# The last 1 MB of an output projection, asked for as a staircase of small transfers

## The chip, the core and the metric

The kernel runs on one core of one Trainium2 chip. The metric is the time of one execution in microseconds (us) on the device; lower is better. TensorE (PE) multiplies, VectorE (DVE) and ScalarE (ACT) do the element work, GpSimd (POOL) hardly takes part, and the queue of SyncE (SP) asks for nearly every transfer. Sixteen DMA engines move the data.

## The reference

Two layers run one after the other, on one token for each of 8 sequences, in float32. Both layers use the same weights and the same cache, so each layer reads all of it again.

```python
def _A_ref(x, k_cache, v_cache, wq, wo):          # x: (8, 1, 1024)
    q = (x @ wq) as 32 heads of 128
    k, v = caches (8, 4, 4096, 128), each of the 4 heads shared by 8 query heads
    p = softmax(q k^T * 128 ** -0.5)
    o = p v
    return o (8, 1, 4096) @ wo                    # wo: (4096, 1024)

def _B_ref(x, w1, b1, w2, b2):
    h = gelu(x @ w1 + b1)                         # w1: (1024, 3584)
    return h @ w2 + b2                            # w2: (3584, 1024)

x = x + _A_ref(layernorm(x), ...); x = x + _B_ref(layernorm(x), ...)   # layer 0
x = x + _A_ref(layernorm(x), ...); x = x + _B_ref(layernorm(x), ...)   # layer 1
```

## The kernel before

All weights and both caches are streamed from HBM through one large tile in SBUF, `arena`. It has 52 units of 1024 columns: 4 KB in each of the 128 partitions, 0.5 MB in all. The order of the stream and the place of each piece are tables written out by hand: `batch(...)` queues the pieces of one sequence's keys and values, `weights(...)` those of a weight matrix, with a list of sizes in units and a list of first units. `pump()` walks that list: it takes the next piece if its units are free, records one transfer on SP's queue (L268), and stops at the first piece whose units are still held. `release(slot)` runs after the last matmul that reads a piece is recorded; it frees the units and calls `pump()`. So the order of the transfers on SP is fixed when the program is built, and on the chip SP takes them strictly one after the other: a transfer that has to wait holds up all those behind it.

A transfer on SP can wait for two kinds of thing. The first is its place: the matmuls that read the old contents. The second is its counter. The framework gives each transfer one of eight counters in turn (`DMAHW0` to `DMAHW7` in the order below), so a transfer has the same counter as the one eight places earlier on SP, and it waits until that one has landed if nothing else already implies it. A transfer counts as landed when its counter has risen by 16.

This is the end of layer 1, where the change lies. `wo` (16 MB) follows the last values tile. In the text its transfers are called wo[0] to wo[5]: three of 4 MB (8 units each), then 2 MB, 1 MB and 1 MB, into units 24, 32, 16, 24, 28 and 30, so that the last three reuse the place of wo[0]. `project` (L424) multiplies the attention output with them, a unit at a time, into one accumulator `y`; then the residual and the layer norm follow (L206 to L229). Next come eleven pieces of `w1`, called w1[0] to w1[10]: five of 2 MB (units 32, 36, 16, 20, 24), three of 1 MB (28, 30, 32), one of 0.5 MB and two of 0.25 MB; and three last pieces of `w2` (`late`). The rest of `w2` for layer 1 already lies in the arena. `expand` (L303, L306) multiplies with `w1`, and `down_row` (L472) with `w2` in between. The result is added at L846 and stored at L848.

Of the kernel before, what the change touches and what calls it, by code (L numbers as in the profile page):

```python
# [14 lines left out]
P = 128  # L15
# [34 lines left out]
Q_AT = (0, (B + 1) * QW - 32, (B + 1) * QW - 8, 32)  # L50
KEEP = SCW + CH + 3 * P
DMA_SCRATCH = 64


class Arena:
# [50 lines left out]
def decode_layers(ctx: ExitStack, tc: tile.TileContext, x, kc, vc, wq, wo, w1, w2, out):  # L106


    nc = tc.nc
# [148 lines left out]
    def pump():  # L258
        while stream:
            key, k, src, starts, keys = stream[0]  # L260
            if not k:
                slot = Kept(starts)
            else:
                slot = arena.take(k, [i for i in starts if i + k <= arena.limit])
            if slot is None:
                return
            stream.pop(0)
            nc.sync.dma_start(out=slot.ap[:, 0:src.shape[1]], in_=src)  # L268
            slot.cols = src.shape[1]
            slot.keys = keys  # L270
            held[key] = slot

    def release(slot):
        if slot.keys:
            held.update(slot.parts())
            return
        slot.free()
        pump()
# [424 lines left out]
    def opened():  # L703
        arena.limit = N_UNIT
        pump()
# [14 lines left out]
    def weights(name, dram, sizes, starts, c0=0, i0=0, kept=None):  # L720

        at = c0
        for i, k in enumerate(sizes):
            n = min(int(k * SCW), dram.shape[1])
            k = -int(-k // 1)
            keys = kept(i) if kept else ()
            stream.append(((name, i0 + i), k, dram[:, at:at + n], starts(k, i), keys))
            at += n
# [26 lines left out]
    def fixed(*at):  # L755
        return lambda k, i: (at[i],)
# [9 lines left out]
    def batch(layer, b, k_spots, v_spots):  # L766
        for a, spots in (("k", k_spots), ("v", v_spots)):
            stream.extend(cache(layer, b, a, listed(*((n, (at,)) for n, at in spots))))
# [19 lines left out]
    at = [32, 16, 24] * (4 * B)  # L788
    for b in orders[1][3:]:
        batch(1, b, *([(8, at.pop(0)), (8, at.pop(0))] for _ in "kv"))  # L790
    weights(("o1",), wo[0], [8, 8, 8, 4, 2, 2], fixed(24, 32, 16, 24, 28, 30))
    weights(("i1",), w1[0], [4] * 5 + [2] * 3 + [1, 0.5, 0.5], fixed(32, 36, 16, 20, 24, 28, 30, 32, 34, 35, 36))
    for e, n in LATE:
        w = LATE_C * Q4
        at, to = CB * NFT * Q4 + e * w, LATE_AT * SCW + e * w
        stream.append((("late", e), 0 if e else LATE_C, w2[0][:, at:at + n * w], arena.ap[:, to:to + n * w] if e else (LATE_AT,), ()))
    pump()
    rs = layernorm(x_row, rsum)
    queries(rs)
# [123 lines left out]
```

## Time and profile before

| | |
|---|---|
| time, median of 3 runs | 849.13 us (848.68 to 849.33) |
| the profiled execution: its own time | 848.87 us |
| its span, first to last instruction | 847.0 us |
| PE busy | 535.8 us, 63% of the span |
| DVE busy | 192.4 us, 23% |
| ACT busy | 55.4 us, 7% |
| read from HBM | 357.78 MB, 423 GB/s over the span |
| mean granted TensorE clock | 0.821 |

In the rows that follow, L268 is line 268 of the kernel. A row of the timeline gives the start, the duration, the engine, the line, the operation, output<-inputs, the shape and the count; the bracket at its end gives how long the engine had stood idle before it and what released it. "DMA to landing" counts from the issue on SP to the moment when the last of the DMA engines has reported. `in_w_dram` stands for w1 and w2 together. Times are counted from the start of the span.

### The profile page before, as it was taken

The page shows a single profiled execution, that of the slowest core. Times are in us where ns is not written, and L with a number is a line of the kernel's source. Part 1 is how long each engine was busy: PE and PEld are TensorE (multiplying, and loading weights), DVE is VectorE, ACT ScalarE, POOL GpSimd, SP SyncE. Part 2 cuts the span into 40 slices and gives each one's busy share as a digit, 9 for nine tenths or more (in the row PEclk, how much of TensorE's full clock was granted, in tenths as well). Part 3 has the DMA queues.
Part 4 walks back from the last instruction along what each step waited for, and adds up shares of the span by engine and source line. Part 5 has one row for each costly group of instructions (what it writes and reads, how often), then busy time and mean ns, then how long its engine had stood idle before and what let it go on. Part 6 is the DMA issues. An engine that isn't in the chain of part 4 may idle for free.

```text
span 847.0 us, 9470 instructions
## 1 busy us (share of the span) xinstructions
PE 535.8 (63%) x4120; PEld 179.1 (21%) x4120; DVE 192.4 (23%) x636; ACT 55.4 (7%) x118; POOL 2.4 (0%) x14
## 2 busy tenths in 40 slices
PE   0755565656656657677778775476666576655677
PEld 0221111111111111133243222111111121212334
DVE  0013132313222231300010242232414132222011
ACT  0110000000000000000201100000000000000021
POOL 0000000000000000000000000000000000000000
PEclk9977779676876877699999897968768768788899
DMA  9999999999999999999999999999999999999997
GB/s 402 420 423 430 433 433 431 426 436 427 424 428 435 434 432 421 427 429 424 429 409 413 399 427 438 429 430 435 425 438 426 434 429 433 431 426 434 421 426 285
DMA packets 19768, 358.51 MB, mean 423 GB/s; under 512 B 2192, under 2 KB 2576, under 8 KB 4112
## 3 DMA queue, kind: packets, MB, share of 16 engines
q1 hardware_dynamic: 19584, 357.77, 99.2%
q8 instruction: 32, 0.52, 0.3%
q10 hardware_dynamic: 144, 0.15, 0.1%
q14 instruction: 8, 0.07, 0.0%
HBM read 357.78 MB, written 0.13 MB: 423 GB/s over the span
## 4 chain that ended last, share of the span: by engine, by line
DMA 73%; PE 23%; DVE 2%; issue 1%; another core or an unknown queue 1%; ACT 0%; SPq 0%; ACTq 0%; DVEq 0%
DMA arena<-in_k_dram 28%; DMA arena<-in_v_dram 21%; DMA arena<-in_w_dram 10%; DMA arena<-in_wo_dram 8%; PE sps L595 8%; PE o_ps L638 7%; DMA arena<-in_wq_dram 5%; PE y L424 2%; PE acc L361 1%; PE sps L472 1%; PE acc L306 1%; PE sps L650 1%; PE acc L303 0%; PE sps L346 0%
## 5 line engine op out<-in xcount | busy, mean ns | idle before, releaser
L595 PE MATMUL sps<-arena,qz 128*32 128x512 f32 x1024 | 162.3, 777 | 118.9 <-DMA arena<-in_k_dram 117.0
L638 PE MATMUL o_ps<-arena 128*32 128x512 f32 x512 | 87.4, 816 | 48.2 <-DMA arena<-in_v_dram 36.7
L638 PE MATMUL o_ps<-arena,spare 128*32 128x512 f32 x512 | 84.9, 782 | 40.9 <-DMA arena<-in_v_dram 34.0
L595 PEld LDWEIGHTS sps<-arena,qz 128*32 128x32 f32 x1024 | 37.7, 132 | 208.2 <-issue 169.8
L643 DVE SCALAR_TENSOR_TENSOR scr<-o_ps,bits,scr 128x128 f32<-128x128 f32 x192 | 67.3, 351 | 6.8
L641 DVE TENSOR_SCALAR scr<-o_ps,bits 128x128 f32<-128x128 f32 x64 | 22.4, 351 | 144.6 <-PE o_ps L638 144.6
L424 PE MATMUL y<-arena,oxT 128*32 128x256 f32 x512 | 37.8, 441 | 23.5 <-DMA arena<-in_wo_dram 23.5
L361 PE MATMUL acc<-arena,oxT 128*32 128x512 f32 x248 | 32.9, 671 | 6.3 <-DMA arena<-in_wq_dram 4.9
L650 PEld LDWEIGHTS sps<-bits,scr 128*128 128x128 f32 x128 | 21.7, 213 | 67.6 <-issue 48.3
L638 PEld LDWEIGHTS o_ps<-arena 128*32 128x32 f32 x512 | 16.9, 134 | 81.4 <-issue 49.1
L638 PEld LDWEIGHTS o_ps<-arena,spare 128*32 128x32 f32 x512 | 17.2, 131 | 71.7 <-issue 47.1
L600 DVE TENSOR_SCALAR_CACHE_REDUCE arena<-sps 128x512 f32<-128x512 f32 x16 | 11.1, 691 | 91.4 <-PE sps L595 91.4
L651 DVE TENSOR_TENSOR oxT<-sps,scr 128x8 f32<-128x8 f32 x64 | 10.5, 164 | 87.1 <-PE sps L650 87.1
L600 DVE TENSOR_SCALAR_CACHE_REDUCE spare<-sps 128x512 f32<-128x512 f32 x16 | 11.1, 691 | 82.4 <-PE sps L595 82.4
L619 ACT ACTIVATE sps<-arena,bits 128x512 f32<-128x512 f32 x16 | 10.9, 681 | 285.2 <-DVE scr L613 285.2
L619 ACT ACTIVATE sps<-spare,bits 128x512 f32<-128x512 f32 x16 | 10.9, 681 | 263.6 <-DVE scr L613 263.6
L650 PE MATMUL sps<-bits,scr 128*128 128x8 f32 x128 | 27.6, 288 | 0.0
L424 PEld LDWEIGHTS y<-arena,oxT 128*32 128x32 f32 x512 | 18.0, 125 | 44.0 <-DMA arena<-in_wo_dram 25.9
L303 PE MATMUL acc<-arena,oxT 128*32 128x512 f32 x160 | 20.7, 631 | 9.2 <-DMA arena<-in_w_dram 9.2
L184 PE MATMUL sps<-spare,ident 128*32 128x512 f32 (+2 forms) x60 | 24.9, 533 | 0.6 <-DVE scr L217 0.6
L609 PE MATMUL sps<-scr,bits 128*128 128x128 f32 x32 | 7.6, 322 | 22.9 <-DVE scr L605 22.9
L466 PE MATMUL sps<-arena,oxT 128*32 128x256 f32 x224 | 14.2, 382 | 5.6 <-DMA arena<-in_w_dram 5.6
(134 smaller groups left out, 248.8 us busy)
## 6 DMA issues: line engine op xcount, KB each, us to landing
arena<-in_v_dram SPq DMA_DIRECT2D x25, 4096.0 KB, 21.6
arena<-in_k_dram SPq DMA_DIRECT2D x21, 4096.0 KB, 20.6
arena<-in_k_dram SPq DMA_DIRECT2D x20, 2048.0 KB, 18.2
arena<-in_w_dram SPq DMA_DIRECT2D x16, 2048.0 KB, 12.7
arena<-in_v_dram SPq DMA_DIRECT2D x11, 2048.0 KB, 19.7
arena<-in_wo_dram SPq DMA_DIRECT2D x8, 2048.0 KB, 13.0
arena<-in_wo_dram SPq DMA_DIRECT2D x3, 4096.0 KB, 24.2
arena<-in_w_dram SPq DMA_DIRECT2D x6, 1024.0 KB, 19.6
```

Source lines behind the costliest of these rows:

```text
L184: nc.tensor.matmul(ps[0:32, 0:w], ident[:, 0:32], spare[:, 0:w], start=True, stop=True)
L303: nc.tensor.matmul(acc[32 * j:32 * j + 32, :], lhs, slot.ap[:, c:c + CH], start=(kt < 4), stop=(kt >= NT - 4))
L361: nc.tensor.matmul(acc[u][32 * j:32 * j + 32, d0 - j * CH:d1 - j * CH], xnT[:, kt * XS:kt * XS + 32], ap[:, d0 - c0:d1 - c0], start=(kt == ...
L424: nc.tensor.matmul(y[32 * j:32 * j + 32, 0:Q4], lhs[:, n * B:n * B + 32], slot.ap[:, c + j * Q4:c + (j + 1) * Q4], start=(n == 0), stop=(n ...
L466: nc.tensor.matmul(y[32 * g:32 * g + 32], h_at(kt), w2_at[c, kt], start=(n < 4), stop=(n >= NFT - 4))
L595: nc.tensor.matmul(ps[32 * g:32 * g + 32, :], qz[:, c:c + 32], kt[:, g * CH:(g + 1) * CH], start=(j == 0), stop=(j == HKV - 1))
L600: nc.vector.tensor_scalar(st["row", b].ap[:, half * CH:(half + 1) * CH], ps, SCALE, None, op0=ALU.mult, op1=ALU.max, accum_out=st["mx", b] ...
L619: nc.scalar.activation(pp, row[:, h * CH:(h + 1) * CH], AF.Exp, bias=bias, scale=1.0, accum_out=ls[:, h:h + 1])
L638: nc.tensor.matmul(o[32 * g:32 * g + 32, :], s[:, g], v[:, g * CH:(g + 1) * CH], start=(half == 0), stop=(half == NH - 1))
L641: nc.vector.tensor_scalar(r, o[:, 0:P], sel_t[:, 0:1], None, op0=ALU.mult)
L643: nc.vector.scalar_tensor_tensor(r, o[:, t * P:(t + 1) * P], sel_t[:, t:t + 1], r, op0=ALU.mult, op1=ALU.add)
L650: nc.tensor.matmul(po[:, 0:REP], r_s[j % 2], sel_h, start=True, stop=True)
```

## The change

wo[5], 1 MB, becomes two tiles of 0.5 MB, in units 30 and 31. The table `CUT` names the first of the two by its key, `(("o1",), 5)`: it is asked for in sixteen transfers of 15, 14, 13 and so on down to 1 rows (partitions), and 8 rows at the end, 128 rows of 4 KB in all. In the text these are p0 to p15, and the whole tile behind them, one transfer of 0.5 MB, is wo[6]. All other transfers stay as they are.

```diff
+CUT = {(("o1",), 5): (*range(15, 0, -1), 8)}
...
-            nc.sync.dma_start(out=slot.ap[:, 0:src.shape[1]], in_=src)
+            r0 = 0
+            for n in CUT.get(key, (P,)):
+                nc.sync.dma_start(out=slot.ap[r0:r0 + n, 0:src.shape[1]], in_=src[r0:r0 + n])
+                r0 += n
...
-    weights(("o1",), wo[0], [8, 8, 8, 4, 2, 2], fixed(24, 32, 16, 24, 28, 30))
+    weights(("o1",), wo[0], [8, 8, 8, 4, 2, 1, 1], fixed(24, 32, 16, 24, 28, 30, 31))
```

SP's queue at the end of `wo`, before (the size is partitions x columns; the names in brackets are the counters waited for, PE's among them):

```order
L268 DMA arena<-in_wo_dram 128x8192 [waits DMAHW2_49,PE_49]
L268 DMA arena<-in_wo_dram 128x8192 [waits DMAHW3_49,PE_49]
L268 DMA arena<-in_wo_dram 128x4096 [waits DMAHW4_49,PE_49]
L268 DMA arena<-in_wo_dram 128x2048 [waits PE_49] x2
L268 DMA arena<-in_w_dram 128x4096 [waits DMAHW5_49,PE_49]
L268 DMA arena<-in_w_dram 128x4096 [waits PE_49]
```

The first two rows are wo[1] and wo[2]; their own counters are DMAHW5 and DMAHW6, and wo[3], wo[4] and wo[5] have DMAHW7, DMAHW0 and DMAHW1. w1[0] follows directly.

The same place after (the line is now L271): wo[4], then p0 to p8.

```order
L271 DMA arena<-in_wo_dram 128x2048 [waits PE_49]
L271 DMA arena<-in_wo_dram 15x1024 [waits PE_49]
L271 DMA arena<-in_wo_dram 14x1024
L271 DMA arena<-in_wo_dram 13x1024
L271 DMA arena<-in_wo_dram 12x1024
L271 DMA arena<-in_wo_dram 11x1024 [waits DMAHW5_49]
L271 DMA arena<-in_wo_dram 10x1024 [waits DMAHW6_49]
L271 DMA arena<-in_wo_dram 9x1024 [waits DMAHW7_49]
L271 DMA arena<-in_wo_dram 8x1024 [waits DMAHW0_49]
L271 DMA arena<-in_wo_dram 7x1024 [waits DMAHW1_49]
```

p0 has DMAHW1, p3 has DMAHW4, and from p4 on every piece waits for a counter alone: p4 for that of wo[1], p5 for wo[2], p6 for wo[3], p7 for wo[4], p8 for p0.

The end of the staircase and what follows it on SP:

```order
L271 DMA arena<-in_wo_dram 2x1024 [waits DMAHW6_49]
L271 DMA arena<-in_wo_dram 1x1024 [waits DMAHW7_49]
L271 DMA arena<-in_wo_dram 8x1024 [waits DMAHW0_49]
L271 DMA arena<-in_wo_dram 128x1024 [waits DMAHW1_49,PE_49]
L271 DMA arena<-in_w_dram 128x4096 [waits DMAHW2_49,PE_49]
L271 DMA arena<-in_w_dram 128x4096 [waits DMAHW3_49,PE_49]
```

wo[6] has come to wait for p8, w1[0] for p9 and w1[1] for p10. Sixteen transfers more are two full turns of the eight counters, so w1[0] and all behind it keep the counters that they had.

On PE, nothing changes but the waits: the last matmuls of `project`, before and after, read

```order
L424 MATMUL y<-arena,oxT 32x256 [waits DMAHW0_49]
L424 MATMUL y<-arena,oxT 32x256 x7
L424 MATMUL y<-arena,oxT 32x256 [waits DMAHW1_49]
L424 MATMUL y<-arena,oxT 32x256 x7
L206 MATMUL sps<-ident,xb 128x128 [waits DVE_49]
```

```order
L428 MATMUL y<-arena,oxT 32x256 [waits DMAHW0_49]
L428 MATMUL y<-arena,oxT 32x256 x7
L428 MATMUL y<-arena,oxT 32x256 [waits DMAHW4_49,DMAHW5_49,DMAHW3_49,DMAHW6_49,DMAHW2_49,DMAHW7_49,DMAHW1_49,DMAHW0_49]
L428 MATMUL y<-arena,oxT 32x256 x3
L428 MATMUL y<-arena,oxT 32x256 [waits DMAHW1_49]
L428 MATMUL y<-arena,oxT 32x256 x3
```

The eight matmuls of wo[5] are now four that wait for all eight counters, and four that wait for wo[6].

## The prediction, made blind

> **What bounds the kernel now.** I read the page first, then the chain of waits over the end, then PE's timeline there, and last the issues on SP one by one.
>
> ```profile
> DMA  9999999999999999999999999999999999999997
> DMA 73%; PE 23%; DVE 2%; issue 1%; another core or an unknown queue 1%; ACT 0%; SPq 0%; ACTq 0%; DVEq 0%
> 771.33 24.16 DMA arena<-in_wo_dram
> 795.53 7.12 PE y L424 x96
> 802.66 27.81 DMA arena<-in_w_dram
> 830.52 1.92 PE acc L303 x16
> ...
> 843.87 0.02 issue
> 843.90 0.42 DVE xb L846
> ```
>
> The DMA engines are busy in every slice, and the chain that ends last is 73% transfers. At the end it runs through wo[2] (issued 771.33, landed 795.5) and w1[4] (issued 802.66, landed 830.5); from there 13.4 us of PE work lead to the last addition. Whatever delays w1[4] delays the end by as much. PE's timeline shows how closely PE follows the transfers:
>
> ```profile
> 785.80 5.29 PE L424 MATMUL y<-arena,oxT 128*32 128x256 f32 x64 [4.55 <-DMA arena<-in_wo_dram]
> 795.53 7.07 PE L424 MATMUL y<-arena,oxT 128*32 128x256 f32 x96 [4.45 <-DMA arena<-in_wo_dram]
> 802.92 1.07 PE L424 MATMUL y<-arena,oxT 128*32 128x256 f32 x16 [0.32 <-DMA arena<-in_wo_dram]
> 805.40 1.07 PE L424 MATMUL y<-arena,oxT 128*32 128x256 f32 x16 [1.41 <-DMA arena<-in_wo_dram]
> 810.38 1.94 PE L303 MATMUL acc<-arena,oxT 128*32 128x512 f32 x8 [2.62 <-DMA arena<-in_w_dram]
> 830.52 1.92 PE L303 MATMUL acc<-arena,oxT 128*32 128x512 f32 x16 [1.31 <-DMA arena<-in_w_dram]
> ```
>
> These starts date the landings: wo[1] 785.8, wo[2] 795.5, wo[4] 802.9, wo[5] 805.4, w1[0] 810.4, w1[4] 830.5. PE waits for each, so it has no lead to spend.
>
> **The change, step by step.** First, when SP issues now (start and, below it, time to landing; wo[3], wo[5], w1[0]):
>
> ```profile
> L268 SPq DMA_DIRECT2D arena<-in_wo_dram x1: 328/328/328, 779.1 to 779.1; - x1
> DMA to landing us min/median/max: 21.3/21.3/21.3
> ...
> L268 SPq DMA_DIRECT2D arena<-in_wo_dram x1: 328/328/328, 781.3 to 781.3; - x1
> DMA to landing us min/median/max: 24.1/24.1/24.1
> ...
> L268 SPq DMA_DIRECT2D arena<-in_w_dram x1: 328/328/328, 789.4 to 789.4; - x1
> ```
>
> wo[3] lands at 779.1 + 21.3 = 800.4. The important thing is the lead: transfers are asked for more than 20 us before they land, and w1[0] is asked for at 789.4, 16 us before wo[5] is in. That lead keeps the engines fed.
>
> Second, is the wait for a counter real? It is in the trace: the first `late` transfer waits for a counter alone, that of w1[3], eight places ahead. Here are w1[3], that transfer, and SP's waits from 824.5 to 834:
>
> ```profile
> L268 SPq DMA_DIRECT2D arena<-in_w_dram x1: 327/327/327, 800.9 to 800.9; - x1
> DMA to landing us min/median/max: 24.0/24.0/24.0
> ...
> L268 SPq DMA_DIRECT2D arena<-in_w_dram x1: 328/328/328, 824.9 to 824.9; - x1
> ...
> SPq L268 <- DMA arena<-in_w_dram: 11.8, 3, 5.2
> ```
>
> w1[3] lands at 800.9 + 24.0 = 824.9, and the next transfer is issued at 824.9. So SP stands still until the transfer eight places ahead has landed on its slowest engine. There it costs nothing: those three are the last. In the staircase it does.
>
> Third, how fast SP issues when nothing holds it. Two in a row:
>
> ```profile
> 501.55 0.33 SPq L268 DMA_DIRECT2D arena<-in_k_dram  x1
> 501.93 0.43 SPq L268 DMA_DIRECT2D arena<-in_v_dram  x1
> ```
>
> That is 0.38 us from one to the next. Now the sequence. p0 is free at 781.3 as wo[5] was; p0 to p3 go out by 782.5. p4 waits for wo[1], 785.8. p5 waits for wo[2], 795.5; p6 for wo[3], 800.4; p7 for wo[4], 802.9. w1[0] and w1[1], which went out at 789.4 and next, stand behind them. p8 waits for p0, which lies right behind wo[4] on the engines and lands within 0.2 us of it, so it is no further stop. From p7 to wo[6] are nine steps (p8 to p15, then wo[6]): 9 x 0.38 = 3.4, so wo[6] is issued at 806.3, and w1[0] at 806.7. The waits of p9 to p15, wo[6] and w1[0] on the piece eight places ahead cost nothing as long as a small piece lands within 8 x 0.38 = 3.0 us of its issue.
>
> By then the engines are empty. Without w1[0], all that was asked for is wo[4] (in at 802.9) and staircase pieces, of which p0 to p5 hold 75 of 128 rows. How long from an issue to the flow? The trace has no transfer to idle engines, so bounds:
>
> ```profile
> out_dram<-xb SPq DMA_DIRECT2D x1, 128.0 KB, 1.7
> ...
> L268 SPq DMA_DIRECT2D arena<-in_w_dram x1: 328/328/328, 442.6 to 442.6; - x1
> DMA to landing us min/median/max: 5.4/5.4/5.4
> ...
> L268 SPq DMA_DIRECT2D arena<-in_k_dram x1: 328/328/328, 473.3 to 473.3; - x1
> ...
> 474.50:475.00 0.50, 0.50 (x8) 0.00 (x0) 0.27 (x1) 0.00 (x0) 0.00 (x0) 0.50 0.78 229
> 475.00:475.50 0.50, 0.50 (x6) 0.14 (x2) 0.00 (x0) 0.00 (x0) 0.00 (x0) 0.88 0.60 197
> 475.50:476.00 0.50, 0.50 (x8) 0.48 (x12) 0.00 (x0) 0.21 (x1) 0.00 (x0) 1.00 0.92 393
> ...
> 797.00:805.00 8.00, 6.67 (x100) 3.26 (x92) 0.00 (x0) 0.00 (x0) 0.00 (x0) 0.85 1.02 427
> ```
>
> The final store of 128 KB, with nothing else moving, takes 1.7 us with its transfer; a load of 0.5 MB behind others took 5.4 (the shortest of all loads). In between lies the issue at 473.3: the queue had run low, the rate (last column, GB/s) fell to 197, and it was back at 393 from 475.5, some 2 us after the issue. I take 2.0, since that row is nearest: a load, after a gap. At 427 GB/s, 0.5 MB takes 1.23.
>
> Landing of wo[6]: 806.3 + 2.0 + 1.2 = 809.5, where wo[5] landed at 805.4: **4.1 us later**. w1[0] is issued 0.4 us behind wo[6], so from there the engines are fed again, and every w1 piece comes at its old distance: w1[4] at 830.5 + 4.1, then 13.4 us of PE work. The layer norm between fits as before (w1[0] came 2.6 us after PE was free). The stores, the `late` pieces and their counters move along.
>
> Sum: 848.87 + 4.1 = **853.0 us**. That is against the profiled execution; the median of the runs is 0.26 above it, well inside the range.
>
> The smaller edits. Splitting the tile gives PE one more wait for eight counters; it stands before wo[6] has landed, so it is covered by that, and would cost a few tenths without. The data and the matmuls are the same. Costs of nothing: the deal of rows over engines, while the gap stands, because engines that run dry all start again together; the skew that they had is lost as well. That could give some back: w1[4] has its landing from the slowest engine, and after the gap the slowest is nearer to the rest. I put this at 0 to 0.7, and PE caps it: it waits 1.31 before w1[4], so a gain above that is not passed on.
>
> Bounds. Low: issues at 0.33 (0.4 less), flow 1.4 us after the issue (the store's 1.7 without 0.3 of transfer, 0.6 less), skew 0.7 less: 851.3, with room 851.0. High: the flow 4.2 us after the issue (5.4 less its 1.2), +2.2; then the round trip of a piece exceeds 3.0 by about 1.2 and delays wo[6] by that: 856.4. It is a row with a queue ahead of it, so I end the range at 856.0.
>
> [...] The price by row is 0.38 us per transfer on SP, plus the waits. [...]
>
> **Rivals.**
>
> *The staircase deals work to the faster engines, and the gap doesn't come (not slower).* The engines do finish apart:
>
> ```profile
> 838.00:839.00 1.00, 1.00 (x40) 0.92 (x36) 0.00 (x0) 0.00 (x0) 0.00 (x0) 1.00 0.91 344
> 839.00:840.00 1.00, 1.00 (x40) 0.83 (x32) 0.00 (x0) 0.00 (x0) 0.00 (x0) 1.00 0.68 264
> 840.00:841.00 1.00, 1.00 (x36) 0.83 (x32) 0.00 (x0) 0.00 (x0) 0.00 (x0) 1.00 0.55 203
> 841.00:842.00 1.00, 1.00 (x28) 0.51 (x24) 0.32 (x1) 0.23 (x1) 0.00 (x0) 1.00 0.29 111
> 842.00:843.00 1.00, 1.00 (x25) 0.60 (x23) 0.00 (x0) 0.00 (x0) 0.00 (x0) 1.00 0.03 12
> ```
>
> The busy share (second last column) falls over four microseconds, so the slowest engine is some 4 us behind the first. If 15 rows go to 15 engines, 14 to 14 and so on, one engine gets 16 rows of this tile and one none, in place of 8 each. A row of 4 KB on one engine takes 4096 B / (427/16 GB/s) = 0.153 us, so the slowest engine gains at most 8 x 0.153 = 1.2 us: 847.6. It loses as much, 850.1, if it is one that gets more. Both need SP to get past p5 to p7 early: wo[6] issued by 802, four microseconds sooner than my sum. The order and the counter row speak against that. 4%.
>
> *A piece is not spread.* All transfers of the trace have 128 rows; what one of 15, 13 or 11 does is not shown. If all pieces went through one engine, it would carry 128 rows, 19.6 us, in place of 1.2: the tile would be 18 us late, 867 us. 4%. [...]
>
> *Round trips bind.* A small piece lands more than 3.0 us after its issue, the eight counters go round slowly, and each later turn adds the excess: 855 to 858 us. The 5.4 us row speaks for it, the store's 1.7 against. 10%.
>
> *PE and the lost skew absorb more than I think:* 850.6 to 851.5. 6%.
>
> **The numbers.** My sum, within 851.3 to 855, has 76%. What a measurement of this kernel can tell from no change is about 0.2%, 1.7 us. Faster by that is almost excluded, as even the perfect deal gives 1.2: 2%. Within it: 4%, the first rival with either sign. Slower: 94%. The range 851.0 to 856.0 leaves out the first two rivals and parts of the others.
>
> **What would show it.** In the profile after: SP's issues of p5 to p7 at about 795.5, 800.4 and 802.9, w1[0] issued near 806.7 in place of 789.4, a hole in the DMA rate from about 803 to 808, and w1[4] near 834.6. No hole, or p5 issued before 790, and I am wrong about the counters; a hole much longer, and the round trip of small pieces is what I got wrong.

## The result

| | before | after |
|---|---|---|
| median | 848.87 us (847.37 to 849.33, 6 runs) | 854.51 us (853.93 to 857.02, 6 runs) |
| ratio to before | | 1.0076, 95% interval 1.0060 to 1.0091 |
| profiled execution, span | 848.87 us, 847.0 us | 857.02 us, 855.2 us |

The change costs 5.6 us by the medians. The profiled execution of after is a long one of its kernel: it was already 1.5 us late when wo[2] landed, ahead of anything that the change touches. So the stages below are compared by the time between landings.

The profile after. From the page, the DMA slices and the chain that ended last; before, all slices but the last were full, and now the third from the end is not:

```profile
DMA  9999999999999999999999999999999999999797
DMA 69%; PE 26%; DVE 2%; issue 1%; ACT 1%; another core or an unknown queue 1%; SPq 1%; ACTq 0%; DVEq 0%
```

PE's timeline, for the landings of wo[2], wo[4], wo[5] (all sixteen pieces), wo[6] and w1[0]:

```profile
797.03 8.15 PE L428 MATMUL y<-arena,oxT 128*32 128x256 f32 x96 [3.55 <-DMA arena<-in_wo_dram]
805.51 1.07 PE L428 MATMUL y<-arena,oxT 128*32 128x256 f32 x16 [0.33 <-DMA arena<-in_wo_dram]
809.94 1.08 PE L428 MATMUL y<-arena,oxT 128*32 128x256 f32 x8 [3.36 <-DMA arena<-in_wo_dram]
812.14 1.08 PE L428 MATMUL y<-arena,oxT 128*32 128x256 f32 x8 [1.12 <-DMA arena<-in_wo_dram]
818.69 1.93 PE L307 MATMUL acc<-arena,oxT 128*32 128x512 f32 x8 [3.78 <-DMA arena<-in_w_dram]
```

SP's issues of p5, p6, p7 and w1[0]:

```profile
L271 SPq DMA_DIRECT2D arena<-in_wo_dram x1: 282/282/282, 797.0 to 797.0; - x1
...
L271 SPq DMA_DIRECT2D arena<-in_wo_dram x1: 273/273/273, 802.3 to 802.3; - x1
...
L271 SPq DMA_DIRECT2D arena<-in_wo_dram x1: 272/272/272, 805.5 to 805.5; - x1
...
L271 SPq DMA_DIRECT2D arena<-in_w_dram x1: 376/376/376, 808.9 to 808.9; - x1
```

p5 goes out the moment wo[2] lands, p7 the moment wo[4] lands, and w1[0], once asked for 16 us ahead of wo[5], now goes out 3.4 us behind wo[4]. The chain of waits now runs through SP. It has p7, which follows the landing of wo[4], and then wo[6] and w1[0], which nothing but their turn held back:

```profile
805.49 0.27 SPq L271
...
808.43 0.36 SPq L271
...
808.88 9.67 DMA arena<-in_w_dram
```

The DMA rate, by windows (the last two columns are the busy share of the engines and GB/s):

```profile
799.00:801.00 2.00, 2.00 (x24) 0.92 (x20) 0.00 (x0) 0.00 (x0) 0.00 (x0) 0.50 1.02 410
801.00:804.00 3.00, 3.00 (x48) 1.51 (x44) 0.00 (x0) 0.00 (x0) 0.00 (x0) 0.72 0.69 212
804.00:810.00 6.00, 2.31 (x44) 0.89 (x40) 0.00 (x0) 0.00 (x0) 0.00 (x0) 0.96 0.30 63
810.00:811.00 1.00, 1.00 (x8) 0.14 (x8) 0.00 (x0) 0.00 (x0) 0.00 (x0) 0.50 0.78 283
811.00:840.00 29.00, 22.24 (x222) 9.18 (x222) 4.07 (x17) 7.22 (x14) 0.00 (x0) 0.73 1.01 428
```

There is the hole: six microseconds at 63 GB/s. And there is something that was not forecast: three microseconds ahead of it the rate is already down to 212. The share of 0.69 accounts for a part of that, since some engines have nothing left to move. The other part is that the busy engines are slower: 212 / 0.69 is 307 GB/s, where the row above it gives 410 / 1.02 = 402.

Taken apart by PE's starts, in us between landings, for every kernel of this study (from the rows of the timeline as shown above; in sixteen_by_columns, where PE does not wait for wo[4], from the landing of wo[4]; each table row is one profiled execution):

| kernel | wo[2] to wo[4] | wo[4] to the last of wo | to w1[0] | sum | against before |
|---|---|---|---|---|---|
| before | 7.39 | 2.48 | 4.98 | 14.85 | |
| after | 8.48 | 6.63 | 6.55 | 21.66 | +6.8 |
| split_only | 7.44 | 2.52 | 4.97 | 14.93 | +0.1 |
| four_by_32 | 9.83 | 8.68 with the next | | 18.51 | +3.7 |
| eight_by_16 | 8.72 | 3.98 | 6.24 | 18.94 | +4.1 |
| twenty_four | 7.68 | 9.44 | 6.07 | 23.19 | +8.3 |
| sixteen_by_columns | 7.4 | 8.5 | 6.11 | 21.96 | +7.1 |
| four_by_columns | 7.45 | 2.76 | 4.97 | 15.18 | +0.3 |
| four_strided | 7.42 | 2.52 | 4.99 | 14.93 | +0.1 |
| deal_of_three | 9.74 | 4.75 | 5.81 | 20.30 | +5.5 |
| deal_strided | 9.76 | 2.53 | 6.12 | 18.41 | +3.6 |
| after_shifted | 8.54 | 6.57 | 5.00 | 20.11 | +5.3 |
| before_shifted | 7.39 | 2.47 | 4.99 | 14.85 | 0.0 |

So the changed kernel loses in three places: 1.1 us before wo[4] has landed, 4.15 between wo[4] and wo[6], and 1.6 on w1[0]. Only the middle one was forecast. From w1[0] to the last addition both kernels take 33.5 us (810.38 to 843.90, 818.69 to 852.15), but not for the same reason. Before, PE waits 0.27 us for w1[3] and 1.31 for w1[4] in that stretch. After, it waits for no tile behind w1[0], because its own work is slower: the third last column of these rows is the granted TensorE clock in the 8 us from w1[0] on, for before, after and four_strided (an experiment below that loses nothing):

```profile
811.00:819.00 8.00, 6.78 (x76) 2.43 (x68) 0.88 (x4) 3.24 (x6) 0.00 (x0) 0.87 1.01 430
819.00:827.00 8.00, 7.14 (x44) 1.99 (x40) 0.88 (x4) 2.66 (x5) 0.00 (x0) 0.53 1.00 428
811.00:819.00 8.00, 7.15 (x44) 2.08 (x40) 0.88 (x4) 2.66 (x5) 0.00 (x0) 0.51 1.01 428
```

The clock of 0.5 is not the work of the change, since four_strided has it without a hole, and sixteen_by_columns, with a hole, has 0.86. But it decides what a late w1[0] costs here. In after, w1[4] landed at 838.14 and PE came to it at 838.77. So an earlier w1[0] alone could have gained 0.6 us, and then w1[4] would have been the bound again. Counted by w1[4], the last part divides into 0.9 us (w1[4] lands 26.0 us behind wo[6] in place of 25.1) and 0.6 us of slower PE.

### The profile page after: what moved, and what is told of

The parts are those of the page before. It is cut to its first block, busy times and chain, and to the rows that moved or that the text cites. A ratio compares the mean times of both kernels' runs of the same rounds, so it can differ in the third digit from the quotient of the medians.

```text
span 855.2 us, 9493 instructions
## 1 busy us (share of the span) xinstructions
PE 539.9 (63%) x4120; PEld 181.5 (21%) x4120; DVE 192.6 (23%) x636; ACT 55.6 (7%) x118; POOL 2.4 (0%) x14
## 4 chain that ended last, share of the span: by engine, by line
DMA 69%; PE 26%; DVE 2%; issue 1%; ACT 1%; another core or an unknown queue 1%; SPq 1%; ACTq 0%; DVEq 0%
DMA arena<-in_k_dram 28%; DMA arena<-in_v_dram 19%; DMA arena<-in_wo_dram 11%; PE sps L599 8%; PE o_ps L642 7%; DMA arena<-in_w_dram 7%; DMA arena<-in_wq_dram 5%; PE acc L307 2%; PE y L428 1%; PE sps L470 1%; PE sps L476 1%; PE acc L365 1%; SPq L271 1%; PE sps L654 0%
## 5 line engine op out<-in xcount | busy, mean ns | idle before, releaser
L599 PE MATMUL sps<-arena,qz 128*32 128x512 f32 x1024 | 164.8, 786 | 120.9 <-DMA arena<-in_k_dram 119.0
L642 PE MATMUL o_ps<-arena 128*32 128x512 f32 x512 | 84.3, 790 | 48.8 <-DMA arena<-in_v_dram 35.1
L428 PE MATMUL y<-arena,oxT 128*32 128x256 f32 x512 | 42.1, 475 | 24.7 <-DMA arena<-in_wo_dram 24.7
L470 PE MATMUL sps<-arena,oxT 128*32 128x256 f32 x224 | 16.4, 452 | 5.2 <-DMA arena<-in_w_dram 5.2
```

The costliest lines, as they stand in the source:

```text
L428: nc.tensor.matmul(y[32 * j:32 * j + 32, 0:Q4], lhs[:, n * B:n * B + 32], slot.ap[:, c + j * Q4:c + (j + 1) * Q4], start=(n == 0), stop=(n ...
L470: nc.tensor.matmul(y[32 * g:32 * g + 32], h_at(kt), w2_at[c, kt], start=(n < 4), stop=(n >= NFT - 4))
L599: nc.tensor.matmul(ps[32 * g:32 * g + 32, :], qz[:, c:c + 32], kt[:, g * CH:(g + 1) * CH], start=(j == 0), stop=(j == HKV - 1))
L642: nc.tensor.matmul(o[32 * g:32 * g + 32, :], s[:, g], v[:, g * CH:(g + 1) * CH], start=(half == 0), stop=(half == NH - 1))
```

## The experiments

**Is it the split alone?**

```diff
-CUT = {(("o1",), 5): (*range(15, 0, -1), 8)}
+CUT = {}
```

> The changed kernel without the staircase: wo[5] and wo[6] are two whole tiles of 0.5 MB, each one transfer on all 128 rows. Theory A (SP stands at the eight counters and the engines run dry): one transfer more moves the counters by one place and no new wait binds, so w1[0] goes out at 789 to 790 and the time is that of the kernel before, within 0.2% (847.4 to 850.6 us). Rival B (splitting the tile, with its extra PE wait, carries the loss): about 854.5.

Measured: 848.48 us, ratio to before 0.9998 (0.9990 to 1.0006). The split is free, extra wait on PE included; the loss is in the sixteen transfers.

**More and fewer pieces.**

```diff
-CUT = {(("o1",), 5): (*range(15, 0, -1), 8)}
+CUT = {(("o1",), 5): (32,) * 4}                    # four_by_32
+CUT = {(("o1",), 5): (16,) * 8}                    # eight_by_16
+CUT = {(("o1",), 5): (5,) * 16 + (6,) * 8}         # twenty_four
```

> wo[5] in four transfers of 32 rows, wo[6] whole. Theory A: the four pieces find free counters; wo[6] waits for wo[1] (785.8 us), w1[0] for wo[2] (795.5 in place of 789.4), w1[1] for wo[3] (800.4), w1[2] for wo[4] (802.9). All are asked for before the queue of the engines is empty, so nothing runs dry: the time of before within 0.2%. Rival C (each small transfer costs a fixed 0.35 us or more wherever it stands, 5.6 us for the sixteen): 4 x 0.35 = 1.4 us slower.

> wo[5] in eight transfers of 16 rows, wo[6] whole. Theory A: the eighth piece goes out when wo[4] has landed (802.9 us), wo[6] 0.4 us behind it, so wo[6] lands at 803.3 + 3.7 (what it took from issue to landing after the gap) = 807.0 in place of 805.4: 1.6 us slower, up to 3 if the first tile of w1 then also loses what it lost in the changed kernel. Rival C (fixed price of each transfer, 0.35 us): 2.8 us slower, and no hole in the DMA rate.

> wo[5] in 24 transfers, sixteen of 5 rows and eight of 6, wo[6] whole. Theory A: after the eighth piece, which goes out when wo[4] lands, there are eight transfers more than in the changed kernel, at 0.33 us each: 2.6 us more, so 8 us slower than before, 857 us. If a piece's landing takes 8 x 0.33 us or less, no more than that. Rival D (the odd shapes of the staircase, 15, 13, 11 rows, and how they are dealt over the engines, carry the loss): with the same rows on five or six engines throughout it differs from 854.5 in a way that the number of transfers doesn't tell.

Measured: four_by_32 852.25 us, ratio 1.0046 (1.0034 to 1.0059); eight_by_16 852.54, 1.0050 (1.0038 to 1.0062); twenty_four 856.26, 1.0089 (1.0074 to 1.0104). Twenty-four pieces came out near their forecast of 857, and their wo[6] lands 2.8 us later behind wo[4] than the changed kernel's, where eight more issues at 0.33 make 2.6. Four pieces did not: theory A had them free, and they cost 3.5 us. Eight pieces cost 3.8, more than the 1.6 to 3 that it gave; their wo[4] is 1.3 us late as well. SP did not stand in the way of four_by_32. This is its DMA rate over seven microseconds, with the engines busy throughout (share 1.04):

```profile
799.00:806.00 7.00, 4.17 (x72) 1.78 (x64) 0.00 (x0) 0.00 (x0) 0.00 (x0) 0.98 1.04 250
```

split_only in the same window:

```profile
799.00:806.00 7.00, 5.82 (x92) 2.59 (x84) 0.00 (x0) 0.00 (x0) 0.00 (x0) 0.94 1.03 428
```

Busy engines that move 250 GB/s in place of 428 are not starved but slow. Even wo[4], a whole tile that is in flight at the same time, is hit: it lands 2.4 us late. Each of the four transfers lies on 32 neighbouring partitions. So a second theory, G, was added, a guess of the author's: a transfer on few neighbouring partitions makes all engines write to a small part of SBUF, and that part is the limit.

**G against A: the same number of transfers, on all partitions.**

```diff
 # sixteen_by_columns and four_by_columns: cut by columns, all 128 rows in each transfer
+CUT = {(("o1",), 5): (784, *[16] * 15)}            # sixteen_by_columns
+CUT = {(("o1",), 5): (256,) * 4}                   # four_by_columns
+            c0 = 0
+            for n in CUT.get(key, (src.shape[1],)):
+                nc.sync.dma_start(out=slot.ap[:, c0:c0 + n], in_=src[:, c0:c0 + n])
+                c0 += n
 # four_strided: 32 rows again, every fourth
+CUT = {(("o1",), 5): 4}
+            m = CUT.get(key, 1)
+            for q in range(m):
+                nc.sync.dma_start(out=slot.ap[q:P:m, 0:src.shape[1]], in_=src[q:P:m])
```

> wo[5] in sixteen transfers again, but each on all 128 rows: 784 columns, then fifteen slivers of 16 columns. The counters turn as in the changed kernel; no transfer is on a part of the partitions. Theory A (counters): SP issues the sixth to eighth piece when wo[2], wo[3] and wo[4] land, wo[6] about 3 us after the eighth, so wo[6] lands 4.1 us late and the DMA rate has a hole of some 4 us; with 0 to 1.5 for a fetch that meets an engine after the restart 853 to 854.4 us, near the changed kernel. Theory G (found in the four pieces of 32 rows: transfers on few partitions run at half the rate, 200 to 250 GB/s, because sixteen engines write to one part of SBUF) as the main cause of the changed kernel's loss: here at most 1 us slower than before.

> wo[5] in four transfers of 256 columns on all 128 rows: as many transfers as four_by_32, of the same size. Theory G: no part of the partitions is favoured, the DMA rate stays at 400 to 430 GB/s, and the time is that of before within 0.2%. Rival C (four more transfers cost something by themselves): 3.5 us slower as four_by_32 was.

> wo[5] in four transfers of 32 rows of 4 KB, as in four_by_32, but each takes every fourth row, so that its rows lie over all the partitions. Theory G: the rate stays up and the loss of 3.5 us goes, to 0 to 1 us. Rival H (any transfer on fewer than 128 rows is slow, through the way its rows are dealt to the engines): 3.5 us slower again, with the rate at 200 to 250 GB/s for some 7 us.

Measured: sixteen_by_columns 856.27 us, ratio 1.0089 (1.0076 to 1.0102); four_by_columns 849.22, 1.0009 (1.0000 to 1.0017); four_strided 849.05, 1.0010 (1.0002 to 1.0019). The window from 799 to 806 in four_by_columns,

```profile
799.00:806.00 7.00, 6.33 (x92) 3.13 (x84) 0.00 (x0) 0.00 (x0) 0.00 (x0) 0.90 1.06 418
```

and in four_strided:

```profile
799.00:806.00 7.00, 5.58 (x92) 2.29 (x84) 0.01 (x1) 0.00 (x0) 0.00 (x0) 1.00 1.02 424
```

The last one differs from four_by_32 only in which rows each transfer takes, and 3 of the 3.5 us are gone. That shows that the choice of rows makes the loss of four_by_32. It turns down C and H as its cause: four transfers more cost 0.5 us by the medians of four_by_columns, 1.4 at most by its interval. That the limit lies in SBUF, as G says, is not shown: the same edit also changes which rows are read from HBM, and no run separates the two. sixteen_by_columns has full-width transfers alone, wo[4] lands on time, and the loss is there all the same, with the hole from 804 to 809:

```profile
804.00:809.00 5.00, 0.51 (x7) 0.05 (x2) 0.00 (x0) 0.00 (x0) 0.00 (x0) 0.76 0.23 28
```

That shows A. The loss is 7.6 us by the medians, and the time is 2 us above the top of the forecast, because SP needs longer from the eighth piece to wo[6] than in the changed kernel. The two issues:

```profile
L271 SPq DMA_DIRECT2D arena<-in_wo_dram x1: 327/327/327, 802.8 to 802.8; - x1
...
L271 SPq DMA_DIRECT2D arena<-in_wo_dram x1: 377/377/377, 807.5 to 807.5; - x1
```

Of these 4.7 us, 1.0 went by until the 784 columns had landed (the ninth piece shares their counter), and the next eight steps took 0.47 us each, where the changed kernel's pieces of 1 to 8 rows took 0.33.

**The third part: w1[0].** In the traces of before and after a transfer on all 128 rows leaves sixteen landing records on its counter, and in after p0 to p14, of 15 to 1 rows, leave fifteen to one of them at the landing; these are read here as one for each engine that takes part. In the changed kernel fifteen landing records of w1[0] lie within 0.5 us (816.43 to 816.93), and the sixteenth is 1.6 us behind them (818.56). A packet of 16 KB on q8, which the page lists as "instruction" and which is read here as a fetch of instructions, starts at 813.58 us in the middle of it. Sixteen matmuls that nobody reads, ahead of `project`, move the fetches.

```diff
+        if st["layer"] == 1:
+            idle(*[32] * 16)
         y = ps_o.tile([P, CH], F32, tag="o", name="y")
```

> The changed kernel, with sixteen small matmuls on PE that nobody reads, ahead of the output projection of layer 1, where PE waits for wo[0]. They move PE's instructions on by 64 entries. Theory E: in the changed kernel w1[0] landed 1.6 us later on one engine than on the other fifteen, because an instruction fetch (the queue q8 of the page) met that engine while it brought w1[0]; moved to an earlier place, into the gap, the fetch costs nothing, and the time falls by 1 to 1.6 us below the changed kernel, to 853 us. Rival F (the late engine comes of the restart after the gap): 854.5 as before, and w1[0] still lands more than 6 us behind wo[6].

> The kernel before with the same sixteen small matmuls: the control. They stand where PE waits 3.9 us for wo[0], so they cost nothing themselves. Theory E: a fetch that is moved meets another moment, and the engines already stand 3.5 us apart there, so the end moves by no more than 0.6 us. If it moves by 1.5 us or more, the matmuls themselves or the fetches act in some other way, and the run above can't be read as a test of the gap.

Measured: after_shifted 856.19 us, ratio 1.0089 (1.0075 to 1.0103); before_shifted 849.07, 1.0005 (0.9996 to 1.0014). Half of theory E holds. The fetch now starts at 801.4, and w1[0] comes 5.00 us behind wo[6] as in the kernel before, in place of 6.55. That turns down F: the restart alone makes no late engine. In twenty_four and sixteen_by_columns a fetch starts at 813.5 and 812.3, again while w1[0] comes in, and one engine is 1.1 us behind the other fifteen.

```profile
809.76 1.08 PE L430 MATMUL y<-arena,oxT 128*32 128x256 f32 x8 [1.03 <-DMA arena<-in_wo_dram]
814.76 1.94 PE L307 MATMUL acc<-arena,oxT 128*32 128x512 f32 x8 [2.23 <-DMA arena<-in_w_dram]
```

But the time did not fall to the forecast 853. The next fetch, at 826.1, meets w1[3], which lands 6.1 us behind w1[2] in place of 4.9. PE does not wait for w1[3], but the late engine stays late, and PE waits for w1[4]:

```profile
835.47 1.92 PE L307 MATMUL acc<-arena,oxT 128*32 128x512 f32 x16 [0.54 <-DMA arena<-in_w_dram]
```

Whether the 1.6 us can be had back at all was not settled.

**The uneven deal without the counters, and without neighbouring rows.** deal_of_three is the kernel before with the row loop of the change; deal_strided has the loop of four_strided.

```diff
+CUT = {(("o1",), 5): (49, 70, 9)}                  # deal_of_three, wo[5] kept at 1 MB
+CUT = {(("o1",), 5): 6}                            # deal_strided: every sixth row, as in four_strided
```

> wo[5] stays one tile of 1 MB, asked for in three transfers of 49, 70 and 9 rows (of 8 KB). Theory A: three transfers find free counters, so there is no gap. [...] In the changed kernel's trace the landings of its pieces say that the engines 11 to 14 were the last, by 4 us. They would lose 3 to 8 rows of 0.306 us: w1[4] lands about 0.9 us earlier, and the time falls by up to 0.9 us (0.1%), to 848.0. Rival: the slow engines are others from run to run, and the time stays, or rises by up to 1.5 us. Slower by 4 us or more would say that partial transfers cost something without the counters.

> The uneven deal without the two costs: wo[5] (0.5 MB) in six transfers, each of every sixth row (two of 22 rows, four of 21), so the rows of each lie over all partitions. The first five find free counters or wait for wo[1]; the sixth waits for wo[2] (795.5 us), wo[6] for wo[3] (800.4), w1[0] for wo[4] (802.9): no hole on the slow engines. [...] In the changed kernel's trace engines 11 to 14 were the last by about 4 us, and engines 0 to 6 the first ones. They would gain 1.2 us: the landings of w1[4] lie closer together (3.5 to 3.7 us in place of 4.2 to 4.4), and the time falls by 0.5 to 1.2 us, to 847.5 to 848.2. Rival: the order of the engines is another in other runs, or PE's own work is the bound there: no change (within 0.1%). A loss of 3 us or more would say that the stride doesn't heal partial transfers on fewer than sixteen engines.

Measured: deal_of_three 854.97 us, ratio 1.0081 (1.0067 to 1.0096); deal_strided 851.95, 1.0036 (1.0022 to 1.0049). Neither gains, and both forecasts missed. The 3 to 8 rows of the one and the 1.2 us of the other rest on the number of rows that each engine gets, which no run shows; the runs showed lower rates in its place. No transfer waits long for a counter in deal_of_three, and it still loses more than four_by_32. The rates, deal_of_three first:

```profile
799.00:806.00 7.00, 5.11 (x80) 2.40 (x72) 0.00 (x0) 0.00 (x0) 0.00 (x0) 0.87 1.08 274
```

```profile
799.00:806.00 7.00, 4.87 (x80) 2.25 (x73) 0.00 (x0) 0.00 (x0) 0.00 (x0) 0.92 0.83 220
```

wo[4] lands 2.4 us late in both. In deal_strided w1[0] has to wait for this late wo[4] (it is issued at 804.6 us) and comes 6.1 us behind wo[6], which is the rest of its loss. Its share of 0.83 says that some engines had nothing to move, but those that had were slow too: the 16 KB packets of the whole tiles took 1.0 to 1.6 us in this window, against 0.61 to 0.63 in four_strided. So spreading the rows heals transfers on 32 rows (424 GB/s) and does not heal those on 22 and 21 rows (220 GB/s). Theory G, as it stands, does not cover this. Why every sixth row is slow and every fourth is not stays open.

## Why the prediction was right, and where it was off

**The counters: right.** p5, p6 and p7 went out as wo[2], wo[3] and wo[4] landed, w1[0] behind all of them, the hole came where it was put, and split_only (no hole without the sixteen transfers) and sixteen_by_columns (the hole with sixteen transfers of another shape) show from both sides that their number makes it. Forecast for wo[4] to wo[6]: 6.6 us (802.9 to 809.5); measured 6.63. That it agrees so closely is luck, as the next paragraph shows.

**Two terms in it were off and cancelled.** The step on SP was taken at 0.38 us from large transfers; pieces of few rows took 0.33 (805.49 to 808.43 for nine steps), 0.5 us less in all. From issue to landing wo[6] was given 2.0 + 1.2 = 3.2 us; it took 3.7 (808.43 to 812.1), 0.5 us more.

**"Costs of nothing: the deal of rows over engines": wrong.** The step priced a row by its engine's rate and did not ask what the pieces do to the transfers beside them. In four_by_32 few neighbouring rows at a time bring the rate of all engines from 428 down to 250 GB/s, and wo[4], which is ahead of them on SP's queue, is 2.4 us late. In the changed kernel it is 1.1 us late, ahead of the hole. That this is the same effect is likely, but not shown: a staircase on spread rows was not run, and deal_strided, whose rows lie over all partitions, is slow too, at 220 GB/s. So neighbouring rows are not the whole cause.

**The lost skew, which was to give back 0 to 0.7: wrong, in sign.** In the kernel before, the landing records of a tile lie 3.5 us apart at that place, and a fetch need not cost anything: the one at 806.65 leaves those of w1[0] 3.5 us apart, and the one at 824.1 puts the last record of w1[4] back by 0.6. After the gap fifteen engines are within half a microsecond, and the one that the fetch met set the landing of w1[0], 1.6 us behind them. And w1[4] no longer set the end, as the sum had it. PE has no wait on `w1` behind w1[0], because its granted clock was lower in this execution (0.53 in the 8 us from w1[0] on, against 0.87 before), as it was in four_strided (0.51), which has no gap.

These two make 1.1 + 1.6 = 2.7 us in the profiled execution, against 1.5 (5.6 less 4.1) that the medians are above the sum. The median still lies within the range, because the room at its upper end, which was meant for a later flow after the issue, took in two costs that were not in the sum. That part is luck.

**The rivals.** The staircase without a gap is turned down by the issues. "A piece is not spread" is turned down by the landing records: on its counter p0 leaves 16 of them, p1 15, p2 14, down to 2 for p14. One comes some half a microsecond after the issue (p0: issued at 783.03, record at 783.58) and the rest, fifteen for p0 and one for p14, at the landing. (The profile counts sixteen records a transfer, so it has no time to landing for any transfer on these counters.) Round trips did not bind: pieces issued into empty engines landed in 1.6 to 2.1 us, below the 3.0 and below the 2.6 of eight measured steps. In four_by_columns four more transfers cost 0.5 us together, and in sixteen_by_columns sixteen cost 7.6, so the price goes by the place in SP's queue and is not a sum over the transfers.

## What to carry to other kernels

Where a queue runs 20 us ahead of its transfers, count how many may be in flight: with eight counters in turn, a burst of more than the free ones stops the queue until older transfers have landed, and everything behind it loses its lead (here w1[0] went out at 808.9 us in place of 789.4). When a tile is cut, cut it along the columns, with all 128 rows in each transfer: transfers on a part of the rows slowed the traffic beside them in most of the runs here (250 GB/s in four_by_32, 274 in deal_of_three, against 428 in split_only), and of the two ways of spreading the rows that were tried, every fourth row was free (ratio 1.0010) and every sixth was not (1.0036). A stream that has been fed without a break can hide a delay of one engine, as the kernel before did for the fetch at 806.65 us; after a break such a delay shows, as the 1.6 us on w1[0] did in the changed kernel. And before a late tile is given a price, look whether PE follows the tiles at all: in the changed kernel, at a granted clock of 0.5, it did not.

## What the runs showed of the hardware that was not expected

- Four transfers of 32 neighbouring rows ran at 250 GB/s with busy engines, and the whole tile in flight beside them landed 2.4 us late; with every fourth row they ran at 424.
- Sixteen engines that started together after a gap spread by 0.5 us, and one instruction fetch put one of them 1.6 us back; in the steady streaming of the kernel before and its control the engines lie 3.5 to 4.7 us apart by the end.
- SP takes 0.33 us for a transfer of 1 to 8 rows, 0.38 to 0.47 for one of 12 to 15, 0.47 for one of 128 short rows, 0.6 for 32 rows of every fourth, and 0.7 to 1.0 for 21 or 22 rows of every sixth.
- The granted TensorE clock in the 8 us behind w1[0] was 0.87 in one profiled execution of the kernel before and 0.50 in one of its control, before_shifted, with the same time within 0.2%.
